# Sending attention output to the second stage in one nine-block DMA transpose per two pairs, and loading the last 64 tokens once per batch

## The chip, the cores and the metric

The kernel runs on one core of a Trainium2 chip. The core has five engines with instruction streams of their own: TensorE (PE in the profile; PEld is its weight load), VectorE (DVE), ScalarE (ACT), GpSimd (POOL) and SyncE (SP), which in this kernel only issues DMAs. Sixteen DMA engines move the data. The metric is the device time of one execution in microseconds (us).

## The reference, cut to what matters

```python
scores = scale * q @ k.T                       # q, k, v: (8 batches, 8 heads, 576 tokens, 64), f32
thresh = scores.max(-1, keepdims=True) - tau
attn   = softmax(where(scores >= thresh, scores, -1e9))
x      = (attn @ v), heads side by side         # (8, 576, 512)
h      = relu(x @ w_in)                        # 512 -> 1024
u, v   = h[..., :512], h[..., 512:]
v_n    = layer-normalise(v)
out    = (u * (w_spatial @ v_n + b_spatial)) @ w_out
```

The first part is attention with a threshold; the second is a gated network (gMLP) over the 576 tokens of each batch, fed with x.

## The kernel before, in words

**Pairs and steps.** Two heads make a *pair*: 32 pairs, four to a batch. 576 tokens are four blocks of 128 and a remainder of 64. A *step* computes the scores of 128 query rows of both heads of a pair against all 576 keys. An even pair has steps 0, 1, 2, 3; an odd pair begins with step 4, which takes the 64 remaining rows of itself and of the even pair before it together, and goes on with 0 to 3. So two pairs take 9 steps, a batch 18, the kernel 144. In what follows the 18 steps of a batch are called *places 0 to 17*: places 0–3 are pair 0 (steps 0–3), 4–8 pair 1 (steps 4, 0, 1, 2, 3), 9–12 pair 2, 13–17 pair 3.

**One step** (`step`, L606). PE writes the scores `s` into one of two large PSUM tiles (L576 four blocks of keys, L580 the remainder). DVE takes the row maxima (L618). ACT writes the exponentials `e` (L641, or L635 and L637 where ACT masks as well). In the next step `mask` (L588) lets DVE zero what lies under the threshold and write `p` (L599; not after steps where ACT did it), and SP sends `p` through a DMA transpose: 18 blocks of 128 x 128 for each two steps (L603, tile `pT`), 9 for a remainder step (L594, tile `ptr`).

**Small jobs inside the steps.** Each step also carries a list `fs` of jobs; each has its matmuls `mm` and its evacuation `ev`. All of them draw their PSUM tile from `bank()`: two small banks (`ps_f`) used in turn, so a job's matmuls wait until the job two before it has been evacuated. The first two jobs run in the middle of the step, the others at its end, before the next step's scores on PE and after the mask on DVE.
- `qk_main`, `qk_rem`: transposes of q and k of the next pair on PE (L246, L261), evacuated by ACT (L251, L253, L264). `qk_rem` runs in steps 1.
- `pv(i, part)`: p times v, two blocks of tokens at once (L290, L295); its `ev` divides on DVE (L302, L304) and writes `xn`.
- `pv_rest(m)`: the same for the 64 remainder rows of pairs 2m and 2m+1, of one 128-row tile; its `ev` writes `xr` (L302, two L304). It runs in step 1 of pair 2m+3, that is at places 6 and 15.
- the gMLP of the batch before: one job a step, in the order `"vsvsvsvssuvuouououo"` from place 8 on (L783): `moe_v` (L436), `moe_s` (L508), `moe_u` (L478), `moe_o` (L537). The last `moe_v` of a batch, at place 0, also runs the end of an earlier batch's output (`ends`, L421 and L424).

**From xn to xT.** x has to be transposed before `moe_v` and `moe_u`. Pairs 0 to 6 and the last two do this on PE (`x_pe`). The other 23 send the four blocks of a pair in a DMA transpose when both its parts are done (L331): the even pair at place 8 or 17, the odd pair at place 4 or 13. The remainder block of two pairs goes in a transpose of its own, 15 in all (L352). `moe_v` first reads xT of a batch at place 8 of the next.

**Loads.** q, k and v of two pairs come in three large DMAs (512 KB each, L109), and their last 64 tokens in four small ones (L116: q, k, v; L120: v's odd heads again, on other partitions). They are put in `queue` when an odd pair starts and are issued one a step. `shape_qk` and `shape_v` on POOL bring q, k and v into the matmuls' layout (L137; L157, L161).

**SP's order.** SP issues its DMAs strictly in program order: within a step the transpose of `p` first, then what `sends` holds (a load, then output and x). The weights w_out come through the same queue, one 256 KB piece in each of four steps (L179), are cast on POOL (L182) and are first used at place 0 of batch 3 (L424).

Of the kernel before, what the change touches and what calls it, by code (L numbers as in the profile page):

```python
# [17 lines left out]
def kernel(  # L18
# [17 lines left out]
    nc = tc.nc  # L36
# [34 lines left out]
    v_ring = [const.tile([P, 11, D + 1], BF16, name=f"v{i}") for i in range(4)]  # L71
    vn_ring = [const.tile([P, 5, 512], BF16, name=f"vn{i}") for i in range(2)]
    ld_ring = [[const.tile([P, 4, n, D], F32, name=f"{t}{i}")
                for t, n in (("ql", 5), ("kl", 4), ("vl", 5))] for i in range(2)]
    vx_ring = [const.tile([P, 2, D], F32, name=f"vx{i}") for i in range(2)]
# [3 lines left out]
    def clear():  # L79
        nc.vector.memset(kd_ring[0], 0.0)  # L80
        nc.gpsimd.memset(ld_ring[0][2][64:128, :, 4, :], 0.0)
        for t in vx_ring:
            nc.gpsimd.memset(t[0:64], 0.0)
        nc.gpsimd.memset(kd_ring[1], 0.0)
        nc.gpsimd.memset(ld_ring[1][2][64:128, :, 4, :], 0.0)
        for t in v_ring:
            nc.vector.memset(t[:, :, D:D + 1], 1.0)
            nc.vector.memset(t[64:128, 4, D:D + 1], 0.0)
            nc.vector.memset(t[0:64, 5, D:D + 1], 0.0)
            nc.vector.memset(t[64:128, 10, D:D + 1], 0.0)  # L90
        for t in vn_ring:
            nc.vector.memset(t[64:128, 4, :], 1.0)
# [9 lines left out]
    def load(i, n, w, eng=nc.sync):  # L102

        b, hp = divmod(i, HP)
        t = ld_ring[i // 2 % 2][w][:, 2 * (i % 2):2 * (i % 2) + 2 * n]
        src = (q, k, v)[w][b, 2 * hp:2 * hp + 2 * n]

        def main():
            eng.dma_start(  # L109
                out=t[:, :, 0:4, :],  # L110
                in_=src[:, 0:512, :].rearrange("h (p c) d -> p h (c d)", c=4))

        def rest():

            u = ld_ring[i // 2 % 2][(0, 0, 2)[w]][(slice(0, 64), slice(64, 128), slice(0, 64))[w]]
            eng.dma_start(out=u[:, 2 * (i % 2):2 * (i % 2) + 2 * n, 4, :],  # L116
                          in_=src[:, 512:576, :].rearrange("h p d -> p h d"))

        def rest_b():
            nc.sync.dma_start(  # L120
                out=vx_ring[i // 2 % 2][64:128],
                in_=src.rearrange("(j h) s d -> h s j d", h=2)[1, 512:576])
        return [main, rest] + ([rest_b] if w == 2 else [])
# [7 lines left out]
    def shape_qk(i):  # L131

        ts = []
        for w, nm in enumerate(("qn", "kn")):
            n = 5 - w
            t = qkn.tile([P, n, 2, D], F32, name=nm)
            nc.gpsimd.tensor_copy(  # L137
                out=t, in_=ld_ring[i // 2 % 2][w][:, 2 * (i % 2):2 * (i % 2) + 2].rearrange(
                    "p h c d -> p c h d"))
            ts.append(t.rearrange("p c h d -> p c (h d)"))  # L140
        nat[i] = ts

    def shape_first():

        qn = qkn.tile([P, 5, 2, D], F32, name="qn")
        kn = qkn.tile([P, 4, 2, D], F32, name="kn")
        for to, t, c, copy in ((qn, 0, slice(0, 4), nc.vector.tensor_copy),
                               (kn, 1, slice(0, 4), nc.scalar.copy),
                               (qn, 0, slice(4, 5), nc.gpsimd.tensor_copy)):
            copy(out=to[:, c], in_=ld_ring[0][t][:, 0:2, c].rearrange("p h c d -> p c h d"))  # L150
        nat[0] = [t.rearrange("p c h d -> p c (h d)") for t in (qn, kn)]

    def shape_v(i):


        j = i % 2
        nc.gpsimd.tensor_copy(  # L157
            out=bass.AP(v_ring[i % 4].tensor, v_ring[i % 4].offset,
                        [v_ring[i % 4].ap[0], [6 * (D + 1), 2], [D + 1, 5], [1, D]]),
            in_=ld_ring[i // 2 % 2][2][:, 2 * j:2 * j + 2])  # L160
        nc.gpsimd.tensor_copy(out=v_ring[i % 4][:, 5, 0:D], in_=vx_ring[i // 2 % 2][:, j, :])  # L161
# [74 lines left out]
    x_on_pe = [j for _, j in x_jobs] + [NPAIR - 2, NPAIR - 1]  # L236

# [18 lines left out]
    def qk_rem(i):  # L256
        hold = {}

        def mm():
            t = hold["t"] = bank()  # L260
            nc.tensor.transpose(out=t[:, 0:P], in_=nat[i][0][:, 4, :], identity=identf)  # L261

        def ev():
            nc.scalar.copy(out=qks[i][:, :, 512:576],  # L264
                           in_=hold["t"][:, 0:P].rearrange("p (w s) -> p w s", w=2))
            kd = kd_ring[i % 2]
            for lo in (0, 64):
                hs = slice(lo, lo + 64)
                nc.gpsimd.tensor_copy(out=kd[hs, hs], in_=qks[i][hs, 1, 512:576])  # L269
        return "act", mm, ev  # L270

    def first():

        qkt = qks[0] = qkT.tile([P, 2, S], F32, name="qkT")
        ts = [ps_s.tile([P, 1536], F32, name="s") for _ in range(2)]
        for t, w, c, at in ([(ts[0], 0, c, c * P) for c in range(5)]
                            + [(ts[1], 1, c, c * P) for c in range(4)]):
            nc.tensor.transpose(out=t[:, at:at + P], in_=nat[0][w][:, c, :], identity=identf)
        nc.scalar.mul(out=qkt[:, 0, 0:512], in_=ts[0][:, 0:512], mul=scale)
        for lo in (0, 64):  # L280
            hs = slice(lo, lo + 64)
            nc.vector.tensor_copy(out=kd_ring[0][hs, hs], in_=ts[0][hs, 576:640])
        nc.scalar.copy(out=qkt[:, 1, 0:256], in_=ts[1][:, 0:256])
        nc.vector.tensor_copy(out=qkt[:, 1, 256:512], in_=ts[1][:, 256:512])
        nc.scalar.copy(out=qkt[:, :, 512:576],
                       in_=ts[0][:, 512:640].rearrange("p (w s) -> p w s", w=2))
# [22 lines left out]
    def pv(i, part):  # L309
# [9 lines left out]
        def ev():  # L319
            if part == 0:  # L320
                xns[i] = xp.tile([P, 4, P], BF16, name="xn")
            xn = xns[i]
            divide(hold["t"], [(slice(0, P), 0, 4,
                                xn[:, 2 * part:2 * part + 2, :].rearrange(
                                    "p c (h d) -> p (c h) d", h=2))])
            if part == 1:
                if hp == 0:
                    xts[b] = xtp.tile([P, 4, 640], BF16, name="xT")
                if i in x_on_pe:
                    return  # L330
                sends.append(lambda: nc.sync.dma_start_transpose(  # L331
                    out=xts[b][:, hp, 0:512].rearrange("p (c s) -> p c s", s=P),
                    in_=xn.rearrange("p c d -> p (c d)")))
        return "dve", mm, ev

    def pv_rest(m):

        b, hp = divmod(2 * m, HP)
# [7 lines left out]
        def ev():  # L346
            xn = xns["rest", m] = xp.tile([P, P], BF16, name="xr")
# [3 lines left out]
            if 2 * m + 1 < NPAIR - 1:  # L351
                sends.append(lambda: nc.sync.dma_start_transpose(  # L352
                    out=xts[b][:, hp, 512:640], in_=xn))
        return "dve", mm, ev

    def rest_of(b, f):

        return xts[b][:, f - f % 2, 512 + 64 * (f % 2):576 + 64 * (f % 2)]

    def x_pe(i, rest=False):  # L360
# [4 lines left out]
        def mm():  # L365
            t = hold["t"] = bank16()
            for c in range(4):
                nc.tensor.transpose(out=t[:, c * P:(c + 1) * P], in_=xns[i][:, c, :],
                                    identity=identb)
            if rest:  # L370
                nc.tensor.transpose(out=t[:, 512:640], in_=xns["rest", i // 2], identity=identb)

        def ev():
            if not rest:
                nc.scalar.copy(out=xts[b][:, hp, 0:512], in_=hold["t"][:, 0:512])
                return
            nc.scalar.copy(out=xts[b][:, hp, 0:256], in_=hold["t"][:, 0:256])
            nc.vector.tensor_copy(out=xts[b][:, hp, 256:512], in_=hold["t"][:, 256:512])
            nc.vector.tensor_copy(out=xts[b][:, hp - 1, 512:640], in_=hold["t"][:, 512:640])
# [47 lines left out]
    def moe_v(b, c):  # L427
        hold = {}

        def mm():  # L430
# [4 lines left out]
            for f in range(4):  # L435
                nc.tensor.matmul(out=t, lhsT=xts[b][:, f, c * P:(c + 1) * P],  # L436
# [34 lines left out]
    def moe_u(b, f):  # L471
        hold = {}

        def mm():
            t = hold["t"] = bank()
            for m in range(4):
                if f < 4:
                    nc.tensor.matmul(out=t, lhsT=w_in[:, m, f * P:(f + 1) * P],  # L478
                                     rhs=xts[b][:, m, 0:512], start=(m == 0), stop=(m == 3))
# [186 lines left out]
    def last_gmlp(b):  # L666

        xt, vn = xts[b], vn_ring[b % 2]
# [3 lines left out]
        for c in range(5):  # L672
            t = bank()
            for f in range(4 if c < 4 else 0):
                nc.tensor.matmul(out=t, lhsT=xt[:, f, c * P:(c + 1) * P],
# [130 lines left out]
    with tc.manual_schedule():  # L806
        for w in (0, 1):
            for f in load(0, 1, w, (nc.sync, nc.scalar)[w]):
                f()
# [6 lines left out]
        for w in (0, 1):  # L816
            for f in load(1, 1, w):
                f()
        for f in load(0, 2, 2):
            f()  # L820
# [9 lines left out]
        for g, (i, c) in enumerate(steps):  # L830
# [4 lines left out]
            if c == 0 and i % 2 and i + 3 < NPAIR or g == 0:  # L835
                for w in range(3):
                    queue.extend(load(i + (3 if g else 2), 2, w))
# [11 lines left out]
            if i % 2 and i > 1 and c == 1:  # L849
# [69 lines left out]
```

## Time and profile before

| what | value |
|---|---|
| time, median of 8 runs | 478.88 us (478.31 to 481.76) |
| the profiled execution | 482.68 us, of which the span from first to last instruction is 480.9 us |
| PE busy | 446.2 us, 93% |
| DVE busy | 411.0 us, 85% |
| ACT busy | 390.9 us, 81% |
| POOL busy | 226.0 us, 47% |
| the SP queue's DMA packets | 225,424, 86.3% of the 16 DMA engines' span |

Busy time is the time in which an engine had an instruction in work. A line of the profile names the line of the kernel, the engine, the operation, then written tile `<-` read tiles. "idle before" is how long the engine stood still before the instruction, and the arrow after it names what ended that.

### The profile page before, as it was taken

Reading aid. Unit: us, or ns where it says so; the run is one execution under the profiler, and the core shown is the slowest. Engines: PE = TensorE matmul, PEld = TensorE weight load, DVE = VectorE, ACT = ScalarE, POOL = GpSimd, SP = SyncE. Lnnn points to the kernel's source line nnn. Section 1 sums busy time; section 2 is a strip of 40 time slices with the busy share of each in tenths; the row PEclk is TensorE's granted clock in tenths of the full one; section 3 lists DMA queues with packets and bytes.
Section 4 is the critical chain, followed back from the end, with each engine's and each line's share of the span. In section 5 each row is a group of like instructions: output and inputs, shape, how many; then the busy total and the mean of one; then the engine's idle time right before and its main releaser. Section 6 shows DMA issues by size and latency. Waiting matters only on the chain.

```text
span 480.9 us, 10926 instructions
## 1 busy us (share of the span) xinstructions
PE 446.2 (93%) x4203; PEld 225.5 (47%) x4203; DVE 411.0 (85%) x563; ACT 390.9 (81%) x677; POOL 226.0 (47%) x403
## 2 busy tenths in 40 slices
PE   7788888889999899999999999999998999999995
PEld 4244444444544445454554545445454545445542
DVE  4889898989889788999889999899888898899573
ACT  4789999999879698788979898789978789797251
POOL 3463334895337643475327652475337544253021
PEclk9799999999999999999999999999999999999999
DMA  7979899969999999898999889988998989677523
GB/s 224 254 158 203 201 221 201 215 142 206 170 195 188 169 214 202 218 156 188 202 185 225 178 200 211 196 176 181 184 213 171 205 185 210 136 114 120 149 85 113
DMA packets 226131, 88.55 MB, mean 184 GB/s; under 512 B 196896, under 2 KB 221600, under 8 KB 226080
## 3 DMA queue, kind: packets, MB, share of 16 engines
q1 hardware_dynamic: 225424, 86.98, 86.3%
q8 instruction: 33, 0.54, 0.5%
q0 software_dynamic: 160, 0.52, 0.3%
q10 hardware_dynamic: 496, 0.36, 0.2%
q14 instruction: 18, 0.15, 0.1%
HBM read 33.31 MB, written 9.44 MB: 89 GB/s over the span
## 4 chain that ended last, share of the span: by engine, by line
PE 43%; DVE 25%; ACT 20%; issue 7%; DMA 3%; POOL 1%; POOLq 0%; ACTq 0%; DVEq 0%
PE s L576 13%; DVE negm L618 12%; DVE p L599 9%; PE s L580 5%; ACT e L641 5%; ACT e L635 5%; PE f L295 4%; PE f L478 3%; PE f L246 3%; ACT p L637 2%; PE f L537 2%; PE f L508 2%; DMA pT<-p 2%; ACT vrel L446 2%; PE f L290 2%
## 5 line engine op out<-in xcount | busy, mean ns | idle before, releaser
L618 DVE TENSOR_REDUCE negm<-s 128x2 f32<-128x1152 f32 x144 | 194.7, 1352 | 35.1 <-PE s L580 34.0
L576 PE MATMUL s<-qkT 64*64 64x512 f32 x1152 | 158.6, 621 | 14.4 <-ACT e L641 8.6
L599 DVE SCALAR_TENSOR_TENSOR p<-e,ctau 128x1152 bf16<-128x1152 f32 x91 | 132.6, 1457 | 1.2 <-ACT e L641 1.2
L641 ACT ACTIVATE e<-s,negm 128x576 f32<-128x576 f32 x182 | 124.9, 741 | 7.2 <-DVE negm L618 6.8
L580 PEld LDWEIGHTS s<-kd,qkT 128*128 128x128 f32 (+1 forms) x320 | 41.6, 178 | 118.4 <-issue 106.3
L635 ACT ACTIVATE e<-s,negm 128x576 f32<-128x576 f32 x106 | 72.9, 742 | 16.4 <-DVE negm L622 11.2
L269 POOL COPY kd<-qkT 64x64 f32<-64x64 f32 x62 | 28.0, 452 | 99.4 <-ACT qkT L264 97.6
L580 PE MATMUL s<-kd,qkT 128*128 128x128 f32 (+1 forms) x320 | 70.1, 323 | 0.0
L576 PEld LDWEIGHTS s<-qkT 64*64 64x64 f32 x1152 | 30.1, 132 | 48.5 <-ACT e L641 18.7
L454 POOL TENSOR_SCALAR nmean<-sm 128x1 f32<-128x1 f32 (+1 forms) x35 | 16.4, 468 | 67.6 <-ACT vrel L446 62.6
L295 PEld LDWEIGHTS <-pT 128*128 128x128 bf16 x1024 | 41.8, 97 | 9.2 <-issue 6.0
L295 PE MATMUL f<-v,pT 128*128 128x65 bf16 x992 | 44.9, 194 | 0.0
L637 ACT ACTIVATE p<-e 128x1152 bf16<-128x1152 f32 x37 | 43.1, 1164 | 1.2
L137 POOL COPY qn<-ql 128x640 f32<-128x640 f32 x31 | 33.8, 1089 | 14.8 <-DVE negm L622 6.0
L290 PE MATMUL f<-v,pT 128*128 128x130 bf16 x124 | 27.2, 219 | 6.1 <-DMA pT<-p 2.6
L466 POOL TENSOR_SCALAR vn<-vrel,rs,nm 128x512 bf16<-128x512 f32 (+1 forms) x34 | 29.6, 871 | 3.7
L508 PE MATMUL f<-wsT,vn 128*128 128x512 bf16 x125 | 31.0, 379 | 0.0
L478 PE MATMUL f<-xT,w_in 128*128 128x512 bf16 x112 | 28.6, 379 | 0.9 <-DVE xn L304 0.8
L436 PE MATMUL f<-w_in,xT 128*128 128x512 bf16 x112 | 28.7, 379 | 0.0
L253 ACT COPY qkT<-f 128x512 f32<-128x512 f32 x31 | 18.3, 589 | 12.7 <-PE f L246 12.1
L304 DVE TENSOR_TENSOR xn<-f,r 128x256 bf16<-128x256 f32 x62 | 26.3, 424 | 2.1
L446 ACT ACTIVATE vrel<-f 128x512 f32<-128x512 f32 (+1 forms) x34 | 20.1, 590 | 8.6 <-PE f L424 4.2
(168 smaller groups left out, 644.0 us busy)
## 6 DMA issues: line engine op xcount, KB each, us to landing
vl<-in_v_dram SPq DMA_DIRECT2D x16, 512.0 KB, 4.4
ql<-in_q_dram SPq DMA_DIRECT2D x15, 512.0 KB, 5.0
kl<-in_k_dram SPq DMA_DIRECT2D x15, 512.0 KB, 4.4
out_dram<-oo SPq DMA_DIRECT2D x10, 512.0 KB, 3.7
uT<-in_moe_w_in_dram SPq DMA_DIRECT2D x3, 512.0 KB, 6.3
uT<-in_moe_w_spatial_dram SPq DMA_DIRECT2D x2, 576.0 KB, 5.5
vl<-in_v_dram SPq DMA_DIRECT2D x16, 64.0 KB, 4.0
pT<-p SPq DMA_TRANSPOSE x64, 5.2
```

Of the source, the lines that this page charges most:

```text
L137: nc.gpsimd.tensor_copy(out=t, in_=ld_ring[i // 2 % 2][w][:, 2 * (i % 2):2 * (i % 2) + 2].rearrange("p h c d -> p c h d"))
L290: nc.tensor.matmul(out=t[:, at:at + 130], lhsT=pt[:, 4, :], rhs=vt[:, 4:6, :].rearrange("p b d -> p (b d)"), start=True, stop=False)
L295: nc.tensor.matmul(out=t[:, at + 65 * h:at + 65 * h + 65], lhsT=pt[:, 5 * h + j, :], rhs=vt[:, 6 * h + j, :], start=False, stop=(h == 1 an ...
L478: nc.tensor.matmul(out=t, lhsT=w_in[:, m, f * P:(f + 1) * P], rhs=xts[b][:, m, 0:512], start=(m == 0), stop=(m == 3))
L508: nc.tensor.matmul(out=t, lhsT=vn[:, c, f * P:(f + 1) * P], rhs=wsT[:, c, 0:512], start=(c == 0), stop=(c == 4))
L576: nc.tensor.matmul(out=s[rows, 1024 * h:1024 * h + 512], lhsT=qks[n][halves[h], 0, m], rhs=qks[n][halves[h], 1, 0:512], start=True, stop=True)
L580: nc.tensor.matmul(out=view(s[rows], 512, [[448, 2], [1, 64]]), lhsT=qks[n][:, 0, m], rhs=kd_ring[n % 2], start=True, stop=True)
L599: nc.vector.scalar_tensor_tensor(out=pt[:, c % 2, :], in0=ef, scalar=ctau, in1=ef, op0=ALU.is_ge, op1=ALU.mult)
L618: nc.vector.tensor_reduce(out=nm, in_=s, axis=AX.X, op=ALU.max, negate=True)
L635: nc.scalar.activation(out=e[:, h, :], in_=s[:, h, :], func=ACT.Prelu, bias=nm[:, h:h + 1], scale=by, alpha=1e30)
L637: nc.scalar.activation(out=pr_ring[i // 2 % 2] if c == 4 else p_ring[2 * (i % 2) + c // 2][:, c % 2], in_=e.rearrange("p h s -> p (h s)"), ...
L641: nc.scalar.activation(out=e[:, h, :], in_=s[:, h, :], func=ACT.Exp, bias=nm[:, h:h + 1])
```

## The change

Nothing that is computed changes. The pieces are cut differently and one job is moved:

- `xn` is now one tile of nine blocks for two pairs: four of the even pair, four of the odd pair, one remainder block. It goes in one DMA transpose when the odd pair is done (places 4 and 13). `xT` has the same nine blocks per two pairs. There are 11 transposes of nine blocks, one of five (pair 6 stays on PE), and three single remainder blocks (m = 0, 1, 2): 15 in place of 38, and 107 blocks as before.
- so that the remainder block is ready by then, `pv_rest(m)` for m = 3 to 14 runs in step 1 of the even pair 2m+2, not of the odd pair 2m+3: at places 1 and 10 in place of 6 and 15. For m = 0, 1, 2 it stays (`rest_late`), since their `ptr` comes from PE later.
- the last 64 tokens of q, k and v are loaded once per batch into tiles of their own (`rest_ring`, `vx_ring`): four DMAs of 128, 128, 64 and 64 KB per batch, in place of eight of 64 or 32 KB. PE transposes the remainder of q and k from there, without a copy on POOL; v's odd heads are no longer loaded twice.
- POOL's copies get shorter (512 columns in place of 640), and the copy of v's remainder becomes two of half the partitions.
- a few clears at the start go or get wider; one copy at the end covers what two did.

```diff
-    v_ring = [const.tile([P, 11, D + 1], BF16, name=f"v{i}") for i in range(4)]
+    v_ring = [const.tile([P, 10, D + 1], BF16, name=f"v{i}") for i in range(4)]
...
-                for t, n in (("ql", 5), ("kl", 4), ("vl", 5))] for i in range(2)]
-    vx_ring = [const.tile([P, 2, D], F32, name=f"vx{i}") for i in range(2)]
+                for t, n in (("ql", 4), ("kl", 4), ("vl", 4))] for i in range(2)]
+    rest_ring = [const.tile([P, H, D], F32, name=f"rl{i}") for i in range(2)]
+    vx_ring = [const.tile([P, HP, D], F32, name=f"vx{i}") for i in range(2)]
...
+    def load_rest(b, w, h0=0, h1=H, eng=nc.sync):
+
+        if w < 2:
+            return lambda: eng.dma_start(
+                out=rest_ring[b % 2][64 * w:64 * w + 64, h0:h1, :],
+                in_=(q, k)[w][b, h0:h1, 512:576, :].rearrange("h p d -> p h d"))
+        return lambda: eng.dma_start(
+            out=vx_ring[b % 2][64 * (w - 2):64 * (w - 2) + 64],
+            in_=v[b].rearrange("(j h) s d -> h s j d", h=2)[w - 2, 512:576])
...
-            nc.tensor.transpose(out=t[:, 0:P], in_=nat[i][0][:, 4, :], identity=identf)
+            nc.tensor.transpose(out=t[:, 0:P], in_=nat_rest(i), identity=identf)
...
-            if part == 0:
-                xns[i] = xp.tile([P, 4, P], BF16, name="xn")
-            xn = xns[i]
...
+            xn = x_nat(i // 2)
+            at = 4 * (i % 2) + 2 * part
...
-                if i in x_on_pe:
-                    return
-                sends.append(lambda: nc.sync.dma_start_transpose(
-                    out=xts[b][:, hp, 0:512].rearrange("p (c s) -> p c s", s=P),
-                    in_=xn.rearrange("p c d -> p (c d)")))
+            elif i not in x_on_pe and i % 2:
+                n0 = 4 if i - 1 in x_on_pe else 0
+                send_x(i // 2, n0, 9)
...
+    def x_nat(m):
+
+        if m not in xns:
+            xns[m] = xp.tile([P, 9, P], BF16, name="xn")
+        return xns[m]
+
+    def send_x(m, n0, n1):
+
+        xn, to = xns[m], xts[m // 2][:, m % 2, n0 * P:n1 * P]
+        sends.append(lambda: nc.sync.dma_start_transpose(
+            out=to.rearrange("p (c s) -> p c s", s=P),
+            in_=xn[:, n0:n1, :].rearrange("p c d -> p (c d)")))
...
-            if 2 * m + 1 < NPAIR - 1:
-                sends.append(lambda: nc.sync.dma_start_transpose(
-                    out=xts[b][:, hp, 512:640], in_=xn))
+            if m in rest_late:
+                send_x(m, 8, 9)
...
                 for w in range(3):
-                    queue.extend(load(i + (3 if g else 2), 2, w))
+                    queue.append(load(n, 2, w))
+                    if n % HP == 0:
+                        queue += [load_rest(n // HP, j) for j in ((0,), (1,), (2, 3))[w]]
...
-            if i % 2 and i > 1 and c == 1:
+            if i > 1 and c == 1 and i % 2 == (i // 2 - 1 in rest_late):
                 small_ones = [pv_rest(i // 2 - 1)]
                 fs += small_ones
```

## The prediction

> **What bounds the kernel now.** I read the table of busy time by stretch first, cut at the batches' ends as the starts of L618 show them.
>
> ```profile
> core 0: us, PE busy (x) PEld busy (x) DVE busy (x) ACT busy (x) POOL busy (x), PEclk, DMA share, GB/s
> 238.80:293.70 54.90, 54.01 (x514) 27.02 (x513) 49.61 (x64) 47.58 (x84) 28.19 (x50) 1.00 0.96 196
> 293.70:348.50 54.80, 53.90 (x513) 26.93 (x512) 49.78 (x64) 47.58 (x84) 28.41 (x49) 1.00 0.93 193
> ```
>
> Two batches, almost the same to the last digit: the starts of L618 are 54.87 us apart from batch to batch. PE is busy for 98% of it, and the DMA engines are too (0.93 to 0.96). So I ask which of the two is waited for, in the list of waits.
>
> ```profile
> PE f L290 <- DMA pT<-p: 2.6, 2, 2.0
> PE f L424 <- POOL w_o L182: 1.8, 1, 1.8
> ```
>
> PE waits for a DMA twice, 2.6 us in all (1.99 of it once, at 371 us), and 1.8 us once for w_out, whose last piece lands at 164.6. In the regular batches nothing on PE waits for a DMA. The chain of waits through such a batch alternates: DVE holds it from 249.9 to 261 us (places 9 to 13), ACT to 267, PE from there on but for one ACT stretch. So what counts is not how busy the queue is, but what is moved within these stretches.
>
> **Part 1: 38 x transposes become 15.** The view of the tiles xT and ptr:
>
> ```profile
> L331 SPq DMA_TRANSPOSE xT<-xn x23: 1212/1259/1474, 126.7 to 433.3; - x23
> L352 SPq DMA_TRANSPOSE xT<-xr x15: 1194/1225/2106, 52.0 to 436.1; - x15
> L594 SPq DMA_TRANSPOSE ptr<-pr x13: 1269/1312/1724, 98.9 to 434.7; - x13
> ```
>
> SP needs 1.26 us to issue four blocks, 1.23 for one, and 1.31 for nine (ptr is the nearest row). So SP saves 23 issues of some 1.25 us, about 29 us, and with four fewer small loads a batch (0.62 us each, 8 batches) another 20, out of some 48.6 us of issuing in each 54.9 us batch. The bytes do not change, and the 256-byte packets hardly (107 blocks either way; the loads save 2,048 of some 190,000). Worth in the sum: 0, since the regular batches have no DMA wait to remove. From both sides: at best the waits quoted above go (-4.4 us), at worst see rival D.
>
> A rule of the Trainium skill speaks against this part: "DMA: Bandwidth & Descriptors", Rules for kernel authors, advises to issue a DMA early and wait for it late. The even pair's x now leaves at place 4 or 13 and not at 17 or 8. The same table says that transfers under 64 KB are mostly overhead, which speaks for it: the single blocks are 32 KB. By the second rule I would expect microseconds, by the trace none.
>
> How late is it? In the regular batch xT of the last pair was issued at 239.23 and landed 3.85 us later, at 243.1; the first matmul that reads it (the fourth of L436, which starts at 245.04) comes at 245.7: 2.6 us of cover. Nine blocks land later by about the difference of ptr's shortest (3.2) and xT's shortest landing (2.4), 0.8 to 0.9; the third matmul needs them too (0.2 earlier), and by part 2 the stretch between shrinks by 0.7. That leaves 0.7 to 0.9 us: 0 in the sum.
>
> **Part 2: pv_rest for m = 3 to 14 moves from places 6 and 15 to places 1 and 10.** This is on the chain. It costs PE 0.71 us (L290 at 238.80 to the next scores at 239.51) and DVE 0.79 (one L302 and two L304, 240.59 to 241.38). I take the four places one at a time; everything before and after is in order on its engine, so a shift is passed on as long as the chain stays on it.
>
> Place 6, removed: on the chain on DVE (p, r, xr, xr, next L618) and on PE. Both move up: **-0.71**.
>
> Place 15, removed. PE in that place:
>
> ```profile
> 265.49 1.24 PE L508 MATMUL f<-wsT,vn 128*128 128x512 bf16 x5
> 267.11 0.22 PE L290 MATMUL f<-v,ptr 128*128 128x130 bf16 x1 [0.38 <-ACT qkT L264]
> ...
> 267.81 1.09 PE L576 MATMUL s<-qkT 64*64 64x512 f32 x8
> ```
>
> pv_rest is the third job of its step and waits for the bank of qk_rem (L264). Without it the scores wait only for the exponentials of the step before last (L641, done at 266.90) and start at 266.95: **-0.86**.
>
> Place 1, added:
>
> ```profile
> 278.48 1.03 PE L478 MATMUL f<-xT,w_in 128*128 128x512 bf16 x4
> 279.87 1.09 PE L576 MATMUL s<-qkT 64*64 64x512 f32 x8 [0.37 <-ACT e L641]
> ```
>
> PE has a hole of 0.37 here, but again it is the third job: its bank comes free when ACT has done L264, which runs from 279.71 to 279.98. PE then works to 280.70, and the scores start there in place of 279.87: about **+0.85**. From 279.87 PE holds the chain for 13 us without a gap, so nothing takes it back.
>
> Place 10, added. DVE there:
>
> ```profile
> 251.87 1.35 DVE L618 TENSOR_REDUCE negm<-s 128x2 f32<-128x1152 f32 x1
> 253.13 1.41 DVE L599 SCALAR_TENSOR_TENSOR p<-e,ctau 128x1152 bf16<-128x1152 f32 x1
> 254.46 1.35 DVE L618 TENSOR_REDUCE negm<-s 128x2 f32<-128x1152 f32 x1
> ```
>
> No idle time is shown: DVE is the chain. The three instructions go between 254.46 and the next L618, which costs at least 0.79. And there is a second wait: moe_s of place 11 (L508, at 254.01) needs the bank that pv_rest leaves, at 255.25. Behind it on PE stand the scores of place 12, the job pv and the scores of place 13; L618 of place 13 gets its scores at 260.9 in place of 259.66: **+1.25**, handed on to ACT.
>
> Sum: 0.85 - 0.71 + 1.25 - 0.86 = +0.53 us a batch, in six batches (m = 3 to 14, two in each): **+3.2 us**. Bounds: if the added parts cost only what PE and DVE lack room for, 0.71 - 0.37 = 0.34 at place 1 and 0.79 at place 10, it is -0.44 a batch, -2.6 in all; if place 15 gives back only its 0.71 and place 10 another 0.3, +1.0 a batch, +6. I take the middle value, which follows the order of instructions.
>
> **Part 3: the rest.** At the start POOL's copy of the remainder (0.29 us, at 5.19) lay before PE's fifth transpose and goes: -0.3 (between 0 and -0.5). The first loads carry 160 KB more ahead of v and w_in, some 0.7 us by the 224 GB/s of that stretch; POOL's 1.0 us idle before v (L157) and more behind it hide that, and if not it costs the 0.7. POOL: qn's copy becomes as short as kn's (1,089 to 647 ns), v's falls from 824 to about 660, and one copy of 381 becomes two of 380 to 450: nothing on balance, with POOL busy half the time; without that cover 0.1 us a pair. The clears change by tenths before the first DMA lands. The end's joined copy (0.29 + 0.21, L378 and L379) lies beside PE's moe_s: 0.
>
> The wait for w_out stays. Its load is behind the transposes of p on SP; SP was up to 1.0 late there (issued at 152.27, p ready at 151.23) and would not be, but p itself comes later by 0.85 - 0.71 + 1.25 = 1.39. So it moves with PE.
>
> **Sum:** +3.2 - 0.3 = +2.9 us. The profiled execution (482.68, of which 480.9 span and 1.8 around it) would give 485.6, less up to 1.2 where the wait at 371 us takes in what place 10 adds. It lies 3.8 above the median, so part of its waits are its own: between 18.7 and 25.6 us, for example, the granted clock was 0.5, and the eight scores matmuls took 1.99 in place of 1.09 us. "TensorE: Matmul & The Clock Gate", part 1, says that this ramp varies from run to run; the diff changes no matmul there. On the median: 478.88 + 2.9 = **481.8**.
>
> **The rivals.** 0.3% is 1.44 us, about what a measurement can tell here; below 477.4 is faster, above 480.3 slower.
> - B, faster: the move evens the load. If banks come free earlier than I read (DVE takes xr before p, or ACT is done sooner since its own stretch moved up), the added parts cost 0.34 + 0.79 against 1.57 saved: 478.88 - 2.6 - 0.3 = **476.0**. It decides as soon as the added parts cost under 1.3 a batch. For it: L290's hole of 0.37 and 0.38 at places 1 and 15. Against: two banks and a fixed order.
> - C, same: half of the bank waits fall away and the move cancels: **478.6**.
> - D, slower still: the nine-block transpose lands after 0.8 us more and moe_v at place 8 stands. At 350.11 xT took 5.05 us to land; with 0.85 more that is over 1 us late. At 0.5 us a batch on top: 481.8 + 3.0 = **484.8**.
> - The change does what it says, but the DMA engines get no rest from it (same packets): that is in all four.
>
> **How the numbers follow.** A (forecast) 0.42, B 0.22, C 0.22, D 0.14. The range from 476.0 to 484.8 leaves out half of B and half of D, 0.18. A's own range is 480.3 to 483.5. Slower: A and D less a little, 0.55; faster: B, 0.22; same 0.23.
>
> **What would show it.** Right: L618 to L618 about 55.4 us a batch; L290 of ptr at place 1 waiting for ACT L264; PE's L508 at place 11 waiting for DVE's xr; SP's issuing down to some 43 us a batch with no change of the time. Wrong: batches shorter than 54.87 (B), or L436 at place 8 waiting for the DMA of xT (D).

## The result, and the profile after

The changed kernel takes **483.93 us** (median of 11 runs, 481.59 to 486.89); the kernel before, run beside it on the same chip, takes 479.45 (32 runs, 478.00 to 483.09). The ratio is 1.009, with a 95% interval of 1.0067 to 1.0113: slower by about 4.5 us. The profiled execution took 485.11 us, of which the span is 483.3.

The table of busy time by stretch, for two stretches of one batch's length:

```profile
core 0: us, PE busy (x) PEld busy (x) DVE busy (x) ACT busy (x) POOL busy (x), PEclk, DMA share, GB/s
239.50:295.20 55.70, 53.94 (x516) 26.95 (x512) 49.59 (x63) 47.47 (x85) 26.57 (x53) 1.00 0.95 192
295.20:350.70 55.50, 53.82 (x516) 26.95 (x512) 49.59 (x63) 47.35 (x85) 26.58 (x53) 1.00 0.96 192
```

The stretches cut through the fifth and the sixth batch, which begin at 222.14 and 277.83 us. These take 55.69 and 55.60 us from L627 to L627, 0.82 and 0.73 more than before, and PE, DVE and ACT have the busy times that they had, within 0.3 us. So the time is added where they stand. The DMA engines are as busy as before, with 23 transposes fewer in all. SP's issuing, added up over the same stretches, falls from some 49 to some 43 us a batch, and nothing comes of it.

The list of waits names who stands for whom (us in total, times, longest):

```profile
PEld L517 <- DVE xn L303: 4.6, 6, 0.8
PE f L289 <- ACT qkT L261: 4.1, 6, 1.5
...
PE f L517 <- DVE xn L303: 3.2, 6, 0.6
...
PEld L445 <- DMA xT<-xn: 2.1, 4, 0.7
```

Line numbers have moved: L517 is `moe_s` (L508 before), L289 the first matmul of `pv` and `pv_rest` (L290), L303 the division that writes `xn` (L304), L261 the copy of `qk_rem` (L264), L445 `moe_v` (L436), L585 and L589 the scores (L576, L580), L627 the row maxima (L618). The wait of `moe_s` for DVE's `xn` comes six times, once in each batch with a moved job; it is new. So is the wait of the loads of L445 for the DMA of `xT`.

PE at place 1 (start us, us, engine, line, ...):

```profile
280.60 1.03 PE L487 MATMUL f<-xT,w_in 128*128 128x512 bf16 x4
282.14 0.22 PE L289 MATMUL f<-v,ptr 128*128 128x130 bf16 x1 [0.52 <-ACT qkT L261]
...
282.85 1.09 PE L585 MATMUL s<-qkT 64*64 64x512 f32 x8
```

`pv_rest` is there as the third job, and it waits for the bank of `qk_rem`, whose copy ACT ends only then. At place 15 it is gone, and nothing but 0.20 us stands between `moe_s` and the scores:

```profile
268.30 1.24 PE L517 MATMUL f<-wsT,vn 128*128 128x512 bf16 x5
269.75 1.09 PE L585 MATMUL s<-qkT 64*64 64x512 f32 x8 [0.20 <-ACT e L650]
```

DVE at place 10, with the three added instructions in two lines, and PE behind it:

```profile
254.64 1.41 DVE L608 SCALAR_TENSOR_TENSOR p<-e,ctau 128x1152 bf16<-128x1152 f32 x1
255.97 0.17 DVE L301 RECIPROCAL r<-f 128x4 f32<-128x4 f32 x1
256.17 0.59 DVE L303 TENSOR_TENSOR xn<-f,r 64x128 bf16<-64x128 f32 x2
256.80 1.36 DVE L627 TENSOR_REDUCE negm<-s 128x2 f32<-128x1152 f32 x1
```

```profile
255.70 0.60 PE L243 MATMUL f<-identf,kn 128*128 128x128 f32 x4
256.82 1.25 PE L517 MATMUL f<-wsT,vn 128*128 128x512 bf16 x5 [0.52 <-DVE xn L303]
```

Before, PE went into the same `moe_s` without a wait:

```profile
254.01 1.24 PE L508 MATMUL f<-wsT,vn 128*128 128x512 bf16 x5
```

Counted from the maxima of place 10, those of place 11 start 0.83 us later than before, and `moe_s` of place 11 starts 1.30 us later (3.45 in place of 2.15). It starts 0.05 us after the second `xn` is written: it takes the bank that `pv_rest` leaves.

The transposes of x, in the view of the tile xT (SP's time to issue one, min/median/max in ns, and the time from issue to landing), and those of the remainder's p in the view of ptr. The first line mixes sizes: the eleven transposes of nine blocks take 1.35 to 1.69 us to issue, the one of five 1.28, the three single blocks 1.21 to 2.29.

```profile
L340 SPq DMA_TRANSPOSE xT<-xn x15: 1212/1558/2289, 52.7 to 436.6; - x15
...
DMA to landing us min/median/max: 2.7/4.0/5.8
```

```profile
L603 SPq DMA_TRANSPOSE ptr<-pr x13: 1291/1363/1932, 101.3 to 438.3; - x13
```

And the chain of waits of the changed kernel at place 8:

```profile
241.37 5.81 DMA xT<-xn
247.17 0.05 issue
247.22 0.60 PE f L445 x2
```

The chain of before had no DMA in its fifth and sixth batch. Here the nine blocks made ready at place 4 are issued at 241.37 and land 5.81 us later, and the last two matmuls of `moe_v` wait for them.

### The profile page after: what moved, and what is told of

The parts are those of the page before. It is cut to its first block, busy times and chain, and to the rows that moved or that the text cites. A ratio compares the mean times of both kernels' runs of the same rounds, so it can differ in the third digit from the quotient of the medians.

```text
span 483.3 us, 10846 instructions
## 1 busy us (share of the span) xinstructions
PE 446.3 (92%) x4203; PEld 226.5 (47%) x4203; DVE 410.9 (85%) x558; ACT 389.9 (81%) x677; POOL 216.8 (45%) x430
## 4 chain that ended last, share of the span: by engine, by line
PE 45%; DVE 22%; ACT 19%; DMA 6%; issue 5%; POOL 1%; SPq 0%; POOLq 0%; ACTq 0%; DVEq 0%
PE s L585 13%; DVE negm L627 9%; DVE p L608 9%; PE s L589 5%; ACT e L650 5%; ACT e L644 4%; PE f L294 4%; PE f L517 4%; PE f L243 3%; PE f L445 3%; PE f L546 2%; DMA xT<-xn 2%; ACT p L646 2%; PE f L487 2%; DVE xn L303 2%
## 5 line engine op out<-in xcount | busy, mean ns | idle before, releaser
L627 DVE TENSOR_REDUCE negm<-s 128x2 f32<-128x1152 f32 x144 | 194.6, 1352 | 37.7 <-PE s L589 37.1
L585 PE MATMUL s<-qkT 64*64 64x512 f32 x1152 | 158.6, 621 | 16.0 <-ACT e L650 9.0
L589 PEld LDWEIGHTS s<-kd,qkT 128*128 128x128 f32 (+1 forms) x320 | 41.6, 179 | 118.4 <-issue 107.9
L589 PE MATMUL s<-kd,qkT 128*128 128x128 f32 (+1 forms) x320 | 70.2, 323 | 0.0
L585 PEld LDWEIGHTS s<-qkT 64*64 64x64 f32 x1152 | 30.1, 132 | 47.8 <-ACT e L650 16.9
L303 DVE TENSOR_TENSOR xn<-f,r 128x256 bf16<-128x256 f32 (+1 forms) x94 | 35.5, 378 | 2.9
L517 PE MATMUL f<-wsT,vn 128*128 128x512 bf16 x125 | 31.1, 379 | 3.2 <-DVE xn L303 3.2
L289 PE MATMUL f<-v,pT 128*128 128x130 bf16 x124 | 27.2, 219 | 5.4 <-ACT qkT L250 2.0
L445 PE MATMUL f<-w_in,xT 128*128 128x512 bf16 x112 | 29.3, 380 | 0.3 <-DMA xT<-xn 0.2
L127 POOL COPY qn<-ql 128x512 f32<-128x512 f32 x31 | 24.6, 795 | 9.1 <-DMA ql<-in_q_dram 7.7
```

The source lines that it names most:

```text
L303: nc.vector.tensor_tensor(out=dst, in0=o[ps, g0:g1, 0:64], in1=r[ps, g0:g1].unsqueeze(2).broadcast_to([ps.stop - ps.start, g1 - g0, 64]), ...
L445: nc.tensor.matmul(out=t, lhsT=x_of(b, f, slice(c * P, (c + 1) * P)), rhs=w_in[:, f, 512:1024], start=(f == 0), stop=(f == 3))
L517: nc.tensor.matmul(out=t, lhsT=vn[:, c, f * P:(f + 1) * P], rhs=wsT[:, c, 0:512], start=(c == 0), stop=(c == 4))
L585: nc.tensor.matmul(out=s[rows, 1024 * h:1024 * h + 512], lhsT=qks[n][halves[h], 0, m], rhs=qks[n][halves[h], 1, 0:512], start=True, stop=True)
L589: nc.tensor.matmul(out=view(s[rows], 512, [[448, 2], [1, 64]]), lhsT=qks[n][:, 0, m], rhs=kd_ring[n % 2], start=True, stop=True)
L627: nc.vector.tensor_reduce(out=nm, in_=s, axis=AX.X, op=ALU.max, negate=True)
```

## The experiments

Each was timed in five rounds beside the kernel before on the same chip. Three groups were run on three occasions; the medians of before were 479.09, 481.11 and 480.64 us, so ratios are to be compared rather than times. "Batch" is the distance between the starts of the row maxima of place 0 in a regular batch (the fifth to the seventh) of the profiled execution, and "place" the same from one place to the next: both are worked out from the starts of L618 or L627 in the trace. Most places repeat to 0.01 or 0.02 us from batch to batch, which a run's time does not; the places at which a DMA is late (8 and 13) do not repeat.

### Each part alone

**The move of pv_rest alone**, in the kernel before:

```diff
-            if i % 2 and i > 1 and c == 1:
+            if i > 1 and c == 1 and i % 2 == (i // 2 - 1 in (0, 1, 2)):
```

> The kernel before, with one thing changed: pv_rest of m = 3 to 14 runs at places 1 and 10 in place of 6 and 15 (x transposes and loads as before). Theory M (the move costs PE and DVE at places 1 and 10 more than it frees at 6 and 15): about +0.7 us a regular batch, in all +3.5 to +4.5 us, that is nearly the whole difference; batches near 55.5 us from L618 to L618. Theory N (the late nine-block transpose costs): 0, batches 54.87 us. Theory L (the loads): 0.

481.31 us, ratio 1.0019 (0.9995 to 1.0043). The trace says more than the ratio: the regular batches take 55.66 us in place of 54.87, each of them, and both predicted waits are there (0.52 us each). The fastest of its 12 runs took 480.69 us, the fastest of the kernel before 476.87. The interval alone would allow no change, and its upper end (+2.1 us) lies below the +3.5 to +4.5 that theory M expected; the 0.79 us a batch is firm.

**Everything but the move** (the changed kernel with `pv_rest` back at places 6 and 15, x in eight blocks for two pairs, and the remainder block alone):

```diff
-                send_x(i // 2, n0, 9)
+                send_x(i // 2, n0, 8)
...
-            if m in rest_late:
+            if 2 * m + 1 < NPAIR - 1:
...
-            if i > 1 and c == 1 and i % 2 == (i // 2 - 1 in rest_late):
+            if i % 2 and i > 1 and c == 1:
```

> The changed kernel with the move taken back: pv_rest always at places 6 and 15, the two pairs' eight blocks in one transpose at places 4 and 13, the remainder block in one of its own (27 x transposes; loads as changed). Theory M: batches back to 54.87 us, the time within 1 us of before. Theory N: eight blocks are nearly as late as nine, so still +0.1 to +0.2 us a batch by the wait at place 8, and nearly the whole +4 us if N were all. Theory L: all that the loads cost stays.

479.86 us, ratio 1.001 (0.9975 to 1.0046); regular batches of 54.87 us, but for the seventh, which takes 55.76 with a wait for a DMA at place 13. Without the move, the change is shown neither to cost nor to bring anything.

**The loads alone** (in the kernel before, the tiles `rest_ring` and `vx_ring`, `load_rest`, and what reads them; x as before):

```diff
+    rest_ring = [const.tile([P, H, D], F32, name=f"rl{i}") for i in range(2)]
+    vx_ring = [const.tile([P, HP, D], F32, name=f"vx{i}") for i in range(2)]
...
+                    if n % HP == 0:
+                        queue += [load_rest(n // HP, j) for j in ((0,), (1,), (2, 3))[w]]
```

> The kernel before with only the loads changed: last 64 tokens once per batch, shorter copies on POOL, new clears; x transposes and pv_rest as before. Theory M and N: 0 to +0.5 us (the first loads carry 160 KB more). Theory L (the first two batches, which are 0.4 and 0.8 us longer in the changed kernel's profile, are so by the loads): +1 to +1.6 us.

478.92 us, ratio 1.0006 (0.9978 to 1.0033); batches of 54.87.

**x and the move, loads as before:**

```diff
-            if part == 0:
-                xns[i] = xp.tile([P, 4, P], BF16, name="xn")
-            xn = xns[i]
+            xn = x_nat(i // 2)
...
+            elif i not in x_on_pe and i % 2:
+                n0 = 4 if i - 1 in x_on_pe else 0
+                send_x(i // 2, n0, 9)
```

> The kernel before with only x changed: nine-block transposes and the move of pv_rest; loads as before. Theory M: +3.5 to +4.5 us, as the move alone. Theory N: more than the move alone by what the wait of L436 for xT at place 8 costs, 0.1 to 0.2 us in each of six batches, so 0.6 to 1.2 us. Theory L: 1 to 1.6 us less than the whole change.

482.71 us, ratio 1.0074 (1.0047 to 1.0101). Batches of 55.63 where the nine blocks land in time, and 56.06 to 56.08 where they do not; the difference lies at place 8 (3.65 us in the first case, 4.12 and 4.09 in the second).

So the move is the larger part of the loss, late x a smaller one, and the loads are neither gain nor loss.

### Taking single suspected costs away

**DVE takes pv_rest ahead of the mask at place 10**, so that its bank comes free for `moe_s` of place 11:

```diff
+        for kind, mm, ev in early:
+            mm()
+            ev()
...
+            early = small_ones if i % 4 == 2 and i > 7 else []
+            fs = [f for f in fs if f not in early]
```

> The changed kernel, but at place 10 DVE evacuates pv_rest before the mask of the step and not after it; the order on PE stays, the amount of DVE work too. Theory M with the bank (moe_s of place 11 waits for the bank that pv_rest leaves): L517's wait of 0.52 us for xn at place 11 goes and a regular batch gets 0.4 to 0.5 us shorter (near 55.2). Rival M without it (DVE's 0.79 us of added work is all that counts there): no change, about 55.6 to 55.7 a batch, +4 us against before.

484.43 us, ratio 1.0073 (1.0045 to 1.0102). The wait of `moe_s` has gone, and the batch is no shorter (55.71 to 55.92). PE now waits for ACT's exponentials before the scores of place 16, 0.73 us where the changed kernel has 0.20:

```profile
267.63 1.02 PE L517 MATMUL f<-wsT,vn 128*128 128x512 bf16 x4
269.38 1.09 PE L585 MATMUL s<-qkT 64*64 64x512 f32 x8 [0.73 <-ACT e L650]
```

So the rival's number came out, but not by the 0.79 us alone. The chain of waits now lies on DVE from place 10 to 263.7 us and on ACT to 269.3, and DVE is held up twice on the way: `p` at place 11 takes 1.77 us (1.40 in the changed kernel), and the small instruction L631 at place 13 takes 0.62 in place of 0.17. The bank wait is real, and taken away in this way it gains nothing; what it costs where it stands is not shown by this run.

**The even pair's four blocks sent alone as before, five blocks with the remainder** (the earlier blocks leave early again):

```diff
-            elif i not in x_on_pe and i % 2:
-                n0 = 4 if i - 1 in x_on_pe else 0
-                send_x(i // 2, n0, 9)
+            elif i not in x_on_pe:
+                send_x(i // 2, 4 * (i % 2), 9 if i % 2 else 4)
```

> The changed kernel, but the even pair's four blocks go on their own when the even pair is done (places 8 and 17, as before the change), and the odd pair's four with the remainder block in a transpose of five at places 4 and 13. pv_rest stays at places 1 and 10. Theory N (the nine blocks land too late for the first moe_v at place 8): place 8 falls back to 3.65 us, the xT wait of L445 goes, 0.1 to 0.4 us a batch and 0.6 to 2 us in all less than the changed kernel. If only the move counts: as the changed kernel, +4 us.

483.00 us, ratio 1.0046 (1.0017 to 1.0075); batches of 55.52 to 55.53, and place 8 back at 3.65. By the batches, the late nine blocks are worth 0.1 to 0.25 us each. In the time the difference to the changed kernel is too small to be told: the intervals overlap.

**The copy of qk_rem at place 1 on DVE**, so that ACT does not hold the bank:

```diff
-            nc.scalar.copy(out=qks[i][:, :, 512:576],
+            copy = nc.vector.tensor_copy if i % 4 == 1 and i > 8 else nc.scalar.copy
+            copy(out=qks[i][:, :, 512:576],
```

> The changed kernel, but at place 1 the copy of qk_rem that pv_rest's bank waits for is made by DVE and not by ACT. Theory M with the bank: the wait of L289 for L261 at place 1 (0.52 us) goes; DVE's copy costs it some 0.3 us before L627, so place 1 gets 0.2 to 0.4 us shorter. Rival: the PE time of pv_rest itself (0.71 us) is what counts, place 1 stays at 3.71.

484.10 us, ratio 1.0076 (1.0043 to 1.0109). PE's wait for that bank has gone, place 0 is 0.38 us longer (2.86 to 3.24), since DVE does the copy ahead of its maxima, and PE now stands 0.82 us for DVE's `xn`. Place 1 is not shorter, as theory M expected, but goes from 3.71 to 3.84. Batches of 55.9 to 56.1: no better.

**All three together:**

```diff
+            copy = nc.vector.tensor_copy if i % 4 == 1 and i > 8 else nc.scalar.copy
...
+            elif i not in x_on_pe:
+                send_x(i // 2, 4 * (i % 2), 9 if i % 2 else 4)
...
+            early = small_ones if i % 4 == 2 and i > 7 else []
```

> The three edits together: early evacuation at place 10, four and five blocks, qk_rem's copy on DVE at place 1. If the three terms add up, a regular batch is 54.8 to 55.0 us, as before the change, and the time within 1 us of before; if a place bound by another engine takes the gains, 55.3 or more and +2 us or more.

485.24 us, ratio 1.0094 (1.0054 to 1.0133), batches of 55.97. Three waits less, two others more (PE's 0.82 us for `xn` and 0.73 for the exponentials, as in the runs above), and no time less. Taken away in these ways, the two bank waits only change into waits for DVE and ACT.

### The two halves of the move

That left the places themselves. In the first group's tables, what the move added at place 1 came back at place 6, and what it added at places 10 and 11 did not come back at 15 and 16. The last group takes the two halves apart.

**From place 15 to place 10 only** (the kernel before, even m from 4 to 14):

```diff
-            if i % 2 and i > 1 and c == 1:
+            if i > 1 and c == 1 and i % 2 == (i // 2 - 1 < 3 or i // 2 % 2 == 0):
```

> Before, with pv_rest moved from place 15 to place 10 only (even m from 4 to 14); odd m stay at place 6; no other part of the change. Theory (the cost of the move lies at place 10, where DVE is the chain): the place table of the move alone gave +0.83 at place 10, +0.50 at place 11 and -0.55 for places 15 and 16 together, so the regular batches take 55.6 us in place of 54.87 (+0.7 to +0.8), and the six batches +3 to +4 on the fastest run of the kernel before. Rival (the two halves share the cost, because the bank wait of place 1 is a loss that place 6 does not give back): about half of it here, 55.2 us a batch and +2 us.

483.12 us, ratio **1.0057** (1.0030 to 1.0085); batches of 55.63. The fastest run is 4.0 us above the fastest of the kernel before.

**From place 6 to place 1 only** (odd m from 3 to 13):

```diff
-            if i % 2 and i > 1 and c == 1:
+            if i > 1 and c == 1 and i % 2 == (i // 2 - 1 < 3 or i // 2 % 2 == 1):
```

> Before, with pv_rest moved from place 6 to place 1 only (odd m from 3 to 13); even m stay at place 15; no other part of the change. Theory: +0.86 at place 1 and -0.83 at place 6 cancel, batches of 54.87 to 54.95 us, the time that of the kernel before within 0.2%. Rival (shared cost): batches of 55.2 us and +2 us.

479.49 us, ratio **0.9978** (0.9947 to 1.0008); batches of 54.89, but for the seventh (56.39, with the wait at place 13). Two kernels with the same amount of work and the same number of moved jobs: one pays 0.76 us a batch, the other 0.02.

**The change with only the free half of the move** (21 transposes of x: those sent at place 4 with nine blocks, those at place 13 with eight, and the remainder block alone):

```diff
-    rest_late = (0, 1, 2)
+    rest_late = (0, 1, 2) + tuple(range(4, 16, 2))
...
-                send_x(i // 2, n0, 9)
+                send_x(i // 2, n0, 8 if i // 2 in rest_late else 9)
```

> The changed kernel with pv_rest moved only where it costs nothing by the theory: odd m at place 1, with x in nine blocks; even m back at place 15, with x in eight blocks and the remainder block alone; 17 + 4 transposes in place of 15 or 38. Theory: batches of 54.9 to 55.1 us (the nine-block transpose that is late at place 8 stays, 0.1 to 0.25), the time that of the kernel before within 0.4%, and some 3 us under the changed kernel of the same call. Rival (late x is what costs): it stays at the changed kernel's time, 55.5 us a batch, since the transpose that place 8 reads is the same nine blocks.

479.81 us, ratio **1.000** (0.9967 to 1.0033); batches of 55.15, 54.89 and 54.90, the first with nine blocks that land late for place 8 (3.91 us).

**The changed kernel once more**, beside these three:

> The changed kernel as it is, beside the three others on the same chip: 0.7 to 1.1% over the kernel before, batches of 55.6 to 55.8 us.

483.68 us, ratio 1.0066 (1.0036 to 1.0095), just under the 0.7% expected; batches of 55.56 to 55.83. The half-moved kernel is 3.9 us below it on the same chip, and as fast as the kernel before. No kernel of the study is shown to be faster than the kernel before.

The table shows where. It gives us from one place to the next, in the same batch (the fifth) of each profiled execution; places 2 and 3 taken together, and the others left out, agree to 0.02.

| place | before | 6 to 1 | 15 to 10 | both moves | the change | half of it |
|---|---|---|---|---|---|---|
| 1 | 2.85 | 3.71 | 2.85 | 3.72 | 3.71 | 3.71 |
| 6 | 3.43 | 2.60 | 3.43 | 2.60 | 2.60 | 2.60 |
| 8 | 3.66 | 3.65 | 3.65 | 3.66 | 3.84 | 3.91 |
| 10 | 2.59 | 2.59 | 3.43 | 3.43 | 3.42 | 2.59 |
| 11 | 3.38 | 3.39 | 3.88 | 3.88 | 3.76 | 3.38 |
| 12 to 14 | 7.73 | 7.73 | 7.73 | 7.73 | 7.83 | 7.73 |
| 15 | 4.06 | 4.06 | 3.24 | 3.25 | 3.22 | 4.06 |
| 16 | 3.68 | 3.68 | 3.94 | 3.94 | 3.83 | 3.68 |
| batch | 54.87 | 54.89 | 55.63 | 55.66 | 55.69 | 55.15 |

The waits of the kernel with the move from 15 to 10 alone, over the last batches, show what is new for PE:

```profile
PE f L508 <- DVE xr L304: 2.1, 4, 0.5
PE f L290 <- DVE gT L525: 0.8, 3, 0.3
```

The first is the bank wait at place 11, 0.52 each time. The second comes at the end of place 16: PE gets to `pv` sooner, since `pv_rest` no longer stands before it, and then waits 0.28 us for DVE's `gT`:

```profile
273.71 0.81 PE L478 MATMUL f<-xT,w_in 128*128 128x512 bf16 x3
274.80 0.22 PE L290 MATMUL f<-v,pT 128*128 128x130 bf16 x1 [0.28 <-DVE gT L525]
```

What makes `gT` late is a small instruction on DVE, L622, which runs after the maxima where ACT masks. Here it is at place 16, first before, then with the job at place 10, with a copy on POOL beside it:

```profile
271.03 0.17 DVE L622 TENSOR_SCALAR negm<-negm 128x2 f32<-128x2 f32 x1
```

```profile
272.11 0.45 DVE L622 TENSOR_SCALAR negm<-negm 128x2 f32<-128x2 f32 x1
271.92 0.61 POOL L137 COPY kn<-kl 128x512 f32<-128x512 f32 x1
```

It ends 0.03 us after the copy. Before, that copy was over 0.4 us ahead of L622. In the 14 profiled executions 183 of these instructions (L622 and its counterparts) take over 0.2 us, and 182 of them end 0.02 to 0.03 us after an instruction of POOL. The drawn-out L622 is the +0.26 of place 16. In the changed kernel POOL's copies are shorter, L631 takes 0.33 there, and place 16 takes 3.83 in place of 3.94.

At place 11 two delays stand side by side. L622 takes 0.64 us there in place of 0.17 (0.53 in the changed kernel), and that is how the +0.50 and +0.38 in the table arise. But PE is late by as much through the job and the bank, runs on without a gap to the scores of place 15, and DVE waits 0.42 us for them there, as before the move (0.43): so PE sets when place 15 begins. No run takes POOL's copy away from L622 alone.

The chain of waits has changed hands in between. In the kernel before, DVE holds it from place 10 on, then ACT into place 15. With the job at place 10, DVE hands it to PE by that bank, and PE carries it without a gap until place 15 begins (the chain of the same kernel; us from the start, us, what):

```profile
255.56 0.31 DVE xr L304
255.86 0.05 issue
255.91 1.25 PE f L508 x5
257.16 1.02 PE s L576 x8
...
266.01 1.02 PE s L576 x8
267.03 0.43 PE s L580 x2
267.46 0.02 issue
267.48 1.22 DVE negm L618
```

## Why the prediction was right, and where its sizes were wrong

The forecast was +2.9 us; the medians differ by 4.5. Sign and mechanism held; the time lies within the range, above A's own 483.5, and nearer to rival D's 484.8 than to the forecast's 481.8. B and C fell with the sign. Step by step:

- **What bounds the kernel** (a chain of PE, DVE and ACT with no DMA in it): held for the kernel before. Busy times are unchanged and the batch is longer. In the changed kernel a DMA comes into the chain at place 8.
- **Part 1 at 0** (fewer transposes): held for the number of issues. The half-moved kernel issues 17 transposes of x fewer, and the small loads of the change, and stands at 1.000; the loads alone stand at 1.0006. The Trainium skill ("DMA: Bandwidth & Descriptors", Rules for kernel authors) says that under 64 KB one pays mostly overhead. The overhead is there (1.2 us of issuing for one block of 32 KB), but no run here gains from saving it; in the fifth and sixth batch of the kernel before no wait for that queue stood on the chain.
- **The cover of 0.7 to 0.9 us at place 8**: this term failed. I let nine blocks land 0.8 to 0.9 us after four. In the last four batches that send them at place 4 they landed 5.5 to 5.8 us after their issue; four blocks took 3.5 to 3.9 us in three of these batches and 5.05 in the fourth: about 2 us more as a rule. So rival D came true in small, and with it a sign that I had named as one of being wrong (`moe_v` at place 8 waiting for xT): 0.1 to 0.3 us a batch (place 8 in the table; the four-and-five kernel takes it away). The row that I used, `ptr`'s shortest landing, was a transpose of nine blocks at another place of the queue; those of x that are sent at place 13 land in 3.4 us as well. The `ptr` transposes issued 1.5 us behind x at the place in question took 3.5 to 5.0 us in the kernel before, and would have been the nearer rows. The number of blocks alone is not it either: without the move, eight blocks sent at place 4 landed after 3.9 to 4.2 us in three of the last four batches (5.7 in the other). What makes the nine late stays open.
- **Place 6, -0.71, and place 1, +0.85**: measured -0.83 and +0.86. The mechanism at place 1 (the third job's bank, held by ACT's L264) is the one seen. The half costs +0.02, where I had +0.14.
- **Place 10, +1.25**: measured +0.84 at place 10 and +0.50 at 11, so 1.34, and on PE, the path that I added up, 1.30 to `moe_s` of place 11 and 1.32 to place 15. The two waits are those named. Not foreseen was that DVE is about as late by then, through L622 beside POOL's copy; rival B let the bank wait fall away, and with the bank free the batch was as long.
- **Place 15, -0.86**: measured -0.82 there, and +0.26 given back at place 16, so -0.56. Here the prediction stopped too early. I followed PE to the scores and took the shift for handed on; I did not ask what is late next: DVE's L622, which stands until POOL's copy ends, and `gT` behind it.
- **Sum +0.53 a batch**: measured +0.79 for the move alone; the half at 10 and 15 is +0.76, where I had +0.39. This is the term of the sum that was mis-sized, by 0.26 us in a regular batch. Over the six batches it is less than six times that, since the last pays only 0.45 (see below). My upper bound, +1.0 a batch, was made with just these two doubts and held it.
- **Part 3, the start at -0.3**: can't be told. The first row maxima start at 9.15 us before and 9.59 after, but at 10.92 in the kernel with the move from 15 to 10 alone, whose start is that of before, and at 10.91 in the changed kernel's second execution.
- **"The wait for w_out stays"**: not settled. PE waited 1.8 us for it in the profiled execution of before, not at all in that of the changed kernel, and 1.8 again in the changed kernel's second one. It comes and goes from run to run.
- **The wait at 371 us "takes in up to 1.2 of place 10"**: the changed kernel's profile shows no wait there, and that batch takes 55.77 in place of 56.90 us. But such waits come and go without the move too (the loads alone had three batches of 54.87 in a row). In the profiled executions of this study, none of the nine with `pv_rest` at place 10 shows a longer place 13 in that batch, and three of the five without it do (5.74, 5.20 and 4.59 us). That the move takes in such waits would fit this, and also that the move alone showed 3.8 us on the fastest run and 2.2 on the median; so few executions are no proof.

The parts come near the total, with late x as one of them. Set against the loads alone, whose profile has no wait at place 13, the six batches with a moved job are longer by 0.67, 0.48, 0.76, 0.76 and 0.77 us with the move from 15 to 10 alone, and by 0.45 in the last (places 0 to 17): 3.9 in all, where the forecast had 3.2. In the changed kernel it is 0.66, 0.45, 0.82, 0.73, 0.90 and 0.72: 4.3 in all, and 4.5 were measured. Of that, place 8 holds some 0.8 in the last four batches, by late x, which the forecast had at 0. These are single executions; the time of the runs alone can't tell late x from zero.

## What to carry to other kernels

When a small job is moved to make a larger transfer possible, price it at the place where it lands and the place it leaves, each on the engine that carries the chain there: here the same job is free from place 6 to 1 and costs 0.76 us a batch from 15 to 10, because at 10 it adds 1.3 us, with the wait for its bank, and at 15 it gives back 0.6 of the 0.8 that it took. Follow the gain past the first instruction that starts earlier, to the first that does not: what is late next takes its share, and it can come from an engine that was not on the chain there, as POOL was not here. And before removing a named wait, ask whether the engine behind it has spare time; the two bank waits removed here gave nothing.

## What the runs showed of the hardware

- **The same DMA transpose lands at different times at different places of a batch.** Nine blocks of x landed 5.5 to 5.8 us after issue when sent at place 4, and after 3.4 when sent at place 13 of the same batches (4.0 in the last); in the half-moved kernel, nine at place 4 took 5.6 to 5.9, eight at place 13 took 3.3 to 3.5 (5.0 in the last batch) and single blocks 2.3 to 2.4 (3.0 for the last). Which of its neighbours does it was not tried.
- **Issuing depends little on the number of blocks**, up to nine: at the median 1.23 us for one block and 1.26 for four in the kernel before, 1.31 for nine there (`ptr`), and 1.35 to 1.69 for nine blocks of x in the changed kernel.
- **A small DVE instruction can stand until a POOL instruction ends.** L622, on 128x2 numbers, takes 0.17 us, and 0.45 or 0.64 beside POOL's copies; 182 of the 183 drawn-out ones in 14 profiled executions end 0.02 to 0.03 us after an instruction of POOL.
- **The granted clock's slow stretches move from run to run.** It was 0.5 from 18.7 to 25.6 us in the profiled execution of before, and from 20.0 to 23.4 and again from 74.6 to 78.0 in that of the changed kernel; in the second execution of the changed kernel it was 0.5 from 168.4 to 171.8 instead, and 1.0 in those two stretches.
